# Attention, then two feed-forward layers on one core: an opening with paired heads in a written order, the first step's points spread out

## The chip, the cores and the metric

The kernel runs on one core of a Trainium2 chip. The metric is device time of one execution in microseconds (us), the median of several runs. Work is done by TensorE (matrix products into the PSUM banks), VectorE, ScalarE, GpSimd (POOL in the rows) and by transfers that SyncE (SP) issues; each engine takes its instructions in the order in which they were written.

## The reference

Three layers follow each other. First chunked attention: 4 batches, 8 heads, 768 positions, head size 64; each chunk of 32 positions sees 8 memory keys, 16 positions to its left, itself and 8 to its right.

```python
for c in range(nc):
    k_full = np.concatenate([mem_k, k_ctx], axis=2)
    v_full = np.concatenate([mem_v, v_ctx], axis=2)
    scores = scale * np.matmul(q_c, k_full.transpose(0, 1, 3, 2))
    scores = scores - np.max(scores, axis=-1, keepdims=True)
    a = np.exp(scores)
    a = a / (np.sum(a, axis=-1, keepdims=True) + 1e-09)
    out[:, :, c_start:c_end] = np.matmul(a, v_full)
```

Its output, 3072 tokens of 512, goes through `relu(x @ w_in)**2 @ w_out` and then, with other weights, through `h * tanh(log1p(exp(h)))` between two such products. `w_in` is 512 x 2048, `w_out` 2048 x 512, all in float64 weights and float32 tokens.

## The kernel before

**Stages.** Tokens are cut into 3 blocks of 1024. A block's attention is done in 4 pairs p of tiles of 128 positions (these are the pairs with numbers below; paired heads are another thing); pairs 0 to 3 (`early(p)`) form the opening, ahead of everything else, and pairs 4 to 7 and 8 to 11 are attended beside the products of the block before. Then 48 steps follow, 24 for each layer, 8 (`NQ`) to a block: step s multiplies the block by 256 columns of `w_in`, applies the gate, and a step later multiplies the result by the matching rows of `w_out`.

**A step.** `product` (L514) computes one of seven products P1 to P7 of sums of blocks of the weights and of x (a Strassen-like scheme), 6 matmuls of 512 columns each, since operands are split into a rounded part and a rest. Their order is P1, P6, P5, P2, P7, P4, P3, onto three PSUM banks a, b, c: P1 and P2 share a, P6, P7 and P4 share b, P5 and P3 share c. P1's bank is copied to u1 by ScalarE before P2 adds onto it; u2 (L817), u3 (L836), c22 (L838), c21 (L844) and c12 (L849) are VectorE sums out of the banks. `gate` runs on ScalarE and the rest of its split on GpSimd (L528). `unit` (L569) multiplies the gated values of the step before by its second matrix, eight units of 6 matmuls, between the products.

**Points.** After each product and each unit `rest()` is called once: it flushes pending stores and does what a table `beside` has planned for that point, 15 points to a step. Step 0 has no units, so points 3 and 4, 7 to 9 and 12 to 14 are called directly after one another. Planned there: the loading and decoding of weights (`plan_w`: A and a decode's first part on ScalarE, D and d its VectorE parts L160, L163 and L164, S and s block sums, R and r rounding on ScalarE L201, L and l the rest on VectorE L207), and attention for later blocks (`plan_attention`): scores at its point 0, maxima at 1 and 2, exponentials (L403, ScalarE) at 3 and 4, normalization (L417, GpSimd) at 6, transposes (L425) at 12, their copy at 13, values (L447) at 16, copy 17, sums 18 (GpSimd), store 22. Pairs 4 to 7 start at point 4 of step 0, then every 24 points.

**The opening** works pair by pair: scores (L367), maximum L385 and subtraction L387 on VectorE, exponentials L399 on ScalarE, sums L411 and inversion L413, L414 on VectorE, normalization L417, transposes L425, copies L435, values L447, copies L459, four sums L466 to L469, and `place_x`, which rounds into x on ScalarE (L479) and writes the rest on VectorE (L480). For each of 4 head groups and 4 chunks the scores are two matmuls, one per head of a pair, on 64 of the 128 rows each; values likewise. `busy(n, i)` issues n dummy matmuls (L872) into bank i.

## Time and profile before

| | us |
|---|---|
| median of three runs | 1082.09 |
| the three runs | 1081.63, 1082.09, 1086.12 |
| the profiled execution's own time | 1084.58 |
| its span, first to last instruction | 1082.8 |
| first product of step 0 starts | 56.40 |
| step 2 starts | 103.64 |

A profile is one execution. Times of rows count from the start of its span; "x12" is the number of instructions that a row merges; the bracket at the end gives the engine's idle time before the row and what ended it.

### The profile page before, as it was taken

Reading aid. Unit: us, or ns where it says so; the run is one execution under the profiler, and the core shown is the slowest. Engines: PE = TensorE matmul, PEld = TensorE weight load, DVE = VectorE, ACT = ScalarE, POOL = GpSimd, SP = SyncE. Lnnn points to the kernel's source line nnn. Section 1 sums busy time; section 2 is a strip of 40 time slices with the busy share of each in tenths; the row PEclk is TensorE's granted clock in tenths of the full one; section 3 lists DMA queues with packets and bytes.
Section 4 is the critical chain, followed back from the end, with each engine's and each line's share of the span. In section 5 each row is a group of like instructions: output and inputs, shape, how many; then the busy total and the mean of one; then the engine's idle time right before and its main releaser. Section 6 shows DMA issues by size and latency. Waiting matters only on the chain.

```text
span 1082.8 us, 19892 instructions
## 1 busy us (share of the span) xinstructions
PE 1042.6 (96%) x7443; PEld 845.8 (78%) x7443; DVE 849.3 (78%) x1147; ACT 586.3 (54%) x1119; POOL 424.3 (39%) x327
## 2 busy tenths in 40 slices
PE   6879999998999999999999999999999999999998
PEld 3658778776778788788888888888888888888887
DVE  5688889869757676789998767787868878867777
ACT  2478667745665764665664654444364443453332
POOL 2224423422333333222232245545465453644443
PEclk9889999999999999999999999999999999999999
DMA  9657877698999998999999998899998899987452
GB/s 346 238 175 275 314 271 273 224 329 295 358 362 323 333 330 281 301 321 380 352 357 323 314 302 279 310 309 339 384 348 289 297 309 365 376 257 224 155 175 78
DMA packets 192143, 321.38 MB, mean 297 GB/s; under 512 B 13488, under 2 KB 151088, under 8 KB 188208
## 3 DMA queue, kind: packets, MB, share of 16 engines
q1 hardware_dynamic: 192048, 320.11, 85.0%
q8 instruction: 60, 0.98, 0.4%
q14 instruction: 35, 0.29, 0.1%
HBM read 228.04 MB, written 92.01 MB: 296 GB/s over the span
## 4 chain that ended last, share of the span: by engine, by line
PE 73%; DVE 10%; ACT 6%; DMA 6%; issue 3%; SPq 2%; POOL 1%; DVEq 0%; ACTq 0%; POOLq 0%
PE banks L514 34%; PE banks L604 20%; PE banks L569 14%; PE banks L447 2%; DMA xt<-xt_d 2%; ACT p L403 1%; DVE y L583 1%; DVE val L163 1%; DVE val L160 1%; DVE val L164 1%; DMA w1s<-w_d 1%; PE banks L367 1%; PE banks L647 1%; ACT r L534 1%; ACT r L533 1%
## 5 line engine op out<-in xcount | busy, mean ns | idle before, releaser
L514 PE MATMUL banks<-x,w1s 128*128 128x512 f32 x2016 | 496.2, 392 | 12.9 <-DVE u L836 5.2
L514 PEld LDWEIGHTS banks<-x,w1s 128*128 128x128 f32 x2016 | 377.9, 189 | 97.7 <-DVE u L836 7.7
L528 POOL TENSOR_TENSOR g<-r,g 128x512 fp32r<-128x512 f32 x190 | 264.0, 1397 | 478.6 <-ACT g L527 346.3
L569 PE MATMUL banks<-g,w2s 128*128 128x512 f32 x1152 | 277.5, 391 | 5.6 <-DVE y L583 4.3
L569 PEld LDWEIGHTS banks<-g,w2s 128*128 128x128 f32 x1152 | 214.6, 188 | 53.8 <-DVE y L583 5.5
L592 DVE TENSOR_TENSOR m<-banks,m 128x1024 f32<-128x1024 f32 (+1 forms) x145 | 175.5, 1214 | 50.8 <-PE banks L604 45.6
L604 PE MATMUL banks<-g,w2s 128*128 128x512 f32 x828 | 206.5, 389 | 0.0
L604 PEld LDWEIGHTS banks<-g,w2s 128*128 128x128 f32 x828 | 155.4, 188 | 32.4
L527 ACT CAST g<-r 128x512 fp32r<-128x512 f32 x190 | 115.7, 620 | 27.9 <-DVE r L555 23.4
L583 DVE TENSOR_TENSOR y<-banks,y 128x512 f32<-128x512 f32 x168 | 111.3, 681 | 21.0 <-PE banks L569 21.0
L528 POOL TENSOR_TENSOR g<-more,g 128x512 fp32r<-128x512 f32 x47 | 66.8, 1426 | 63.3 <-ACT g L527 42.2
L533 ACT ACTIVATE r<-r 128x512 f32<-128x512 f32 x72 | 45.4, 630 | 56.0 <-DVE r L844 40.2
L537 ACT ACTIVATE r<-r 128x512 f32<-128x512 f32 x48 | 30.3, 632 | 72.1 <-DVE r L844 37.3
L534 ACT ACTIVATE r<-r 128x512 f32<-128x512 f32 x96 | 60.8, 633 | 3.0
L160 DVE TENSOR_SCALAR val<-val 128x512 f32<-128x512 f32 x64 | 40.3, 630 | 18.8 <-ACT val L153 18.8
L226 DVE TENSOR_TENSOR val<-val,hi 128x1024 f32<-128x1024 f32 (+1 forms) x32 | 35.7, 1116 | 23.8 <-ACT hi L219 23.5
L219 ACT CAST hi<-val 128x1024 fp32r<-128x1024 f32 (+1 forms) x32 | 30.5, 952 | 39.1 <-DVE val L164 19.3
L153 ACT ACTIVATE val<-raw 128x512 f32<-128x512 f32 x64 | 40.4, 668 | 20.7 <-DMA w_d<-val 10.0
L810 ACT COPY u<-banks 128x512 f32<-128x512 f32 x48 | 28.3, 589 | 41.3 <-PE banks L514 41.3
L164 DVE SCALAR_TENSOR_TENSOR val<-raw,val 128x512 uint32<-128x512 uint32 x64 | 47.2, 737 | 2.2
L417 POOL TENSOR_TENSOR p<-p,sum 128x512 f32<-128x512 f32 x22 | 28.2, 1301 | 43.8 <-DVE sum L414 22.0
L836 DVE TENSOR_TENSOR u<-banks,u 128x512 f32<-128x512 f32 x48 | 33.0, 688 | 12.7 <-PE banks L514 9.9
(88 smaller groups left out, 1044.6 us busy)
## 6 DMA issues: line engine op xcount, KB each, us to landing
w1s<-w_d SPq DMA_DIRECT2D x280, 256.0 KB, 6.0
w2s<-w_d SPq DMA_DIRECT2D x229, 256.0 KB, 5.9
raw<-w_dram SPq DMA_DIRECT2D x64, 512.0 KB, 5.6
w_d<-w1s SPq DMA_DIRECT2D x8, 1792.0 KB, 7.4
x<-xs_d SPq DMA_DIRECT2D x14, 1024.0 KB, 11.1
v<-v_dram SPq DMA_DIRECT2D x24, 512.0 KB, 8.2
xt<-xt_d SPq DMA_DIRECT2D x21, 512.0 KB, 8.2
k<-k_dram SPq DMA_DIRECT2D x24, 368.0 KB, 7.2
```

Of the source, the lines that this page charges most:

```text
L153: nc.scalar.activation(out=val, in_=high.bitcast(FP32), func=ACTF.Prelu, scale=REBIAS, alpha=NEGATIVE)
L160: nc.vector.tensor_scalar(out=val, in0=val, scalar1=LIMIT, scalar2=-LIMIT * NEGATIVE, op0=ALU.min, op1=ALU.max)
L164: nc.vector.scalar_tensor_tensor(out=vb, in0=low, scalar=29, in1=vb, op0=ALU.logical_shift_right, op1=ALU.bitwise_or)
L514: nc.tensor.matmul(out=ps, lhsT=w[:, a, f:f + 128], rhs=x[:, xi, c, kk, :], start=start and i == 0, stop=stop and i == len(order) - 1, ski ...
L527: nc.scalar.copy(out=g[:, 0], in_=r)
L528: nc.gpsimd.tensor_tensor(out=g[:, 1], in0=r, in1=g[:, 0].bitcast(FP32), op=ALU.subtract)
L533: nc.scalar.activation(out=r, in_=h, func=ACTF.Relu)
L534: nc.scalar.activation(out=r, in_=r, func=ACTF.Square)
L569: nc.tensor.matmul(out=ps, lhsT=w[:, a, blk(f), d % 2 * 128:d % 2 * 128 + 128], rhs=g_t[s, (f, t)][:, c, :], start=i == 0, stop=i == len(o ...
L583: nc.vector.tensor_tensor(out=y, in0=ps, in1=y, op=ALU.add)
L592: engine.tensor_tensor(out=to, in0=in0, in1=in1, op=ALU.add)
L604: nc.tensor.matmul(out=bank(first + d), lhsT=w[:, a, 128 * d:128 * d + 128], rhs=g[:, c, :], start=i == 0 and blk not in ONTO, stop=i == 2 ...
```

## The change

The opening is rewritten, and the first two steps and the first planned attention are moved.

- The two heads of a pair are multiplied together: K is laid into zeroed tiles, block-diagonally (`pairs_k`), so that one matmul uses all 128 rows and gives both heads' 64 slots; the transposed probabilities are laid out in the same way (`pairs_p`) for the values. VectorE and GpSimd zero the tiles at the start, K is loaded in four transfers a pair and not two, and each half's probabilities are copied by two ScalarE instructions of 64 rows.
- Scores, softmax, sums, normalization, transposes, values and placing are called by halves, in one order written as a string: a letter for the work, then the pair and the half. `place_x`'s rest of pair 0 (l00, l01) goes to GpSimd, block sums of pair 2 too. There are fewer dummy matmuls.
- In step 0 each product is followed by two points (`tick`), and P2 comes second.
- The second matrix of step 0 is decoded from point 9 and not 4, and step 1's eight units stand after P7 (four) and after P3 (four).
- Pairs 4 to 7 are attended from point 10, every 23 points; transposes and what follows them stand one point later, as they already did for pairs 8 to 11.

```diff
+        for j in range(2):
+            for i in range(2):
+                r = slice(64 * i, 64 * i + 64)
+                nc.sync.dma_start(
+                    out=pairs_k[p % 2][j][r, i], in_=k[2 * p + j][r].rearrange("p (a s) -> p a s", a=4)
+                )
...
+    def lay_pairs():
+        both = pool.tile([128, 2, 2, 4, KCOLS], FP32, tag="w1_1", name="kk")
+        pairs_k.append([pool.tile([128, 2, 4, KCOLS], FP32, tag=f"y{j}", name="kk") for j in range(2)])
+        pairs_k.append([both[:, j] for j in range(2)])
+        pairs_p.extend(pool.tile([128, 4, 4, 2, 32], FP32, tag=f"g{4 + j}", name="pp") for j in range(2))
+        for n, engine in enumerate((nc.vector, nc.gpsimd)):
+            for j in range(2):
+                for i in range(2):
+                    engine.memset(pairs_k[n][j][64 - 64 * i:128 - 64 * i, i], 0.0)
+        for j in range(2):
+            for i in range(2):
+                nc.gpsimd.memset(pairs_p[j][64 - 64 * i:128 - 64 * i, :, :, i], 0.0)
...
+    def scores_pairs(p, j):
...
+        for hp in range(4):
+            for c in range(4):
+                nc.tensor.matmul(
+                    out=out4[32 * c:32 * c + 32, hp // 2, :, hp % 2],
+                    lhsT=q_t[p][:, j, hp, 32 * c:32 * c + 32],
+                    rhs=pairs_k[p % 2][j][:, :, hp, STRIDE * c:STRIDE * c + SLOTS],
...
+        if early(p):
+            for j in halves:
+                ps = s_ps.pop((p, j)).rearrange("p (a c s) -> p a c s", a=4, c=4)
+                for i in range(2):
+                    r = slice(64 * i, 64 * i + 64)
+                    nc.scalar.copy(out=pairs_p[j][r, :, :, i], in_=ps[r])
+            return
...
+                    for c in range(4):
+                        for i in range(2):
+                            nc.tensor.matmul(
+                                out=to[64 * i:64 * i + 64, :, 1 - j, 32 * c:32 * c + 32],
+                                lhsT=v_t[p][j][:, i, a, c, :],
+                                rhs=pairs_p[j][:, 2 * a + i, c],
+                            )
...
-            12 + late: lambda: transpose_p(p),
-            13 + late: lambda: (copy_pt(p), load_q(p + 1) if (p + 1) % PSB else None),
-            16 + late: lambda: values(p),
-            17 + late: lambda: copy_x(p),
-            18 + late: lambda: sums_x(p, nc.gpsimd),
+            13: lambda: transpose_p(p),
+            14: lambda: (copy_pt(p), load_q(p + 1) if (p + 1) % PSB else None),
+            17: lambda: values(p),
+            18: lambda: copy_x(p),
+            19: lambda: sums_x(p, nc.gpsimd),
...
-                units_of(((), (), (0, 1), (), (2, 3, 4), (5, 6, 7))[n])
+                units_of((((), (), (0, 1), (), (2, 3, 4), (5, 6, 7)), ((), (), (), (), range(4), range(4, 8)))[s == 1][n])
...
+        def tick():
+            rest()
+            if s == 0:
+                rest()
...
+            if s == 0:
+                product(s, P2, a, False, True)
+                tick()
+                gate(s, 0, 0, a, new_r(layer))
             product(s, P6, b, True, False)
-            rest()
+            tick()
...
+        work = {
+            "s": scores_pairs, "x": softmax, "e": exps, "u": total, "i": invert,
+            "n": lambda p, j: divide(p, j, on["PPPD"[p]]),
+            "t": transpose_p, "c": copy_pt, "v": values, "o": copy_x,
+            "m": lambda p, i: sums_x(p, on["PPPD"[p]], i),
+            "h": lambda p, half: place_x(p, half, 0),
+            "l": lambda p, half: place_x(p, half, 1, on["PDDD"[p]]),
+            "b": busy,
...
+            "b12,7 s00 s01 Q2 K2 W0 W1 V1 x00 x01 e00 b3,2 s10 u00 e01 s11 Q3 K3 V2 V3 u01 i0 x10 n00 n01"
+            " b5,4 t00 x11 e10 c00 b1,5 t01 u10 b1,6 s20 e11 c01 s21 x20 v00 u11 e20 v01 A0 i1 x21 n10 A1 o00"
+            " n11 b1,2 t10 D1 o01 e21 m00 b1,2 t11 c10 u20 u21 m01 h00 b2,2 v10 i2 c11 D0 s30 n21 h01 v11 n20"
+            " S0 R0 l00 t21 x30 o11 s31 c21 t20 x31 l01 o10 e30 b1,0 v21 S1 e31 c20 u31 u30 m10 R1 b3,0 v20"
+            " i3 n30 h10 m11 L0 b1,0 t30 o21 o20 n31 c30 m20 L1 b2,0 t31 h11 v30 l10 m21 c31 l11 h20 b2,0 v31"
+            " l20 o31 o30 h30 m30 h21 l30 m31 l21 h31 l31 b9,0"
...
-                plan_w(s, 4, (0, s, 1), "A||a|D|d||R||L", round_w, split_w, "xt2")
+                plan_w(s, 4 if s else 9, (0, s, 1), "A||a|D|d||R||L", round_w, split_w, "xt2")
...
-            start, first, period = ((0, 4, 24), (NQ, 10, 22))[sb]
+            start, first, period = ((0, 10, 23), (NQ, 10, 22))[sb]
```

## Rows read from the trace of the kernel before

**Rows 1.** The profile page, busy time of each engine.

```profile
PE 1042.6 (96%) x7443; PEld 845.8 (78%) x7443; DVE 849.3 (78%) x1147; ACT 586.3 (54%) x1119; POOL 424.3 (39%) x327
```

**Rows 2.** Table by stages: PE, PEld, DVE, ACT, POOL busy, granted clock, DMA share, GB/s.

```profile
40.00:50.00 10.00, 7.77 (x146) 6.12 (x145) 7.82 (x14) 4.42 (x8) 0.00 (x0) 0.68 0.70 249
...
600.00:700.00 100.00, 100.00 (x443) 82.81 (x442) 75.96 (x87) 52.29 (x78) 45.99 (x33) 1.00 0.89 298
```

**Rows 3.** Timeline of TensorE, opening to step 2: start, length, line, count.

```profile
6.86 1.63 PE L367 MATMUL banks<-k,q 64*32 64x64 f32 x128
...
16.77 1.04 PE L425 MATMUL banks<-cst,p 128*128 128x128 f32 x8
...
20.23 2.06 PE L447 MATMUL banks<-pt,v 64*64 64x32 f32 x124 [0.17 <-ACT pt L435]
...
59.94 4.72 PE L514 MATMUL banks<-x,w1s 128*128 128x512 f32 x12 [1.81 <-ACT x L479]
...
78.30 2.93 PE L514 MATMUL banks<-x,w1s 128*128 128x512 f32 x6 [4.09 <-DVE r L844]
...
103.64 4.24 PE L514 MATMUL banks<-x,w1s 128*128 128x512 f32 x18
```

**Rows 4.** The chain that ended last, step 0: start, length, instruction.

```profile
72.36 4.86 ACT p L403 x32
```

**Rows 5.** The waits from 100 to 340 us: total, times, longest.

```profile
PEld banks L425 <- POOL p L417: 4.0, 4, 1.3
```

**Rows 6.** Timelines of SP and ScalarE in steps 6 and 7.

```profile
218.53 0.42 SPq L473 DMA_DIRECT2D xt_d<-stage  x1
...
222.47 0.33 SPq L137 DMA_DIRECT2D w_d<-w1s  x1
...
227.08 2.94 SPq L267 DMA_DIRECT2D xt<-xt_d  x2
...
237.12 1.05 ACT L281 CAST x<-xt 128x1024 fp32r<-128x1024 f32 x1 [8.59 <-DMA xt<-xt_d]
```

**Rows 7.** Timeline of VectorE, opening and step 0.

```profile
8.52 0.69 DVE L385 TENSOR_REDUCE mx<-banks 128x8 f32<-128x512 f32 x1 [6.59 <-PE banks L367]
...
11.18 1.47 DVE L411 TENSOR_REDUCE sum<-p 128x8 f32<-128x512 f32 x2
...
12.89 0.25 DVE L414 RECIPROCAL sum<-sum 128x16 f32<-128x16 f32 x1
...
59.92 1.23 DVE L480 TENSOR_TENSOR x<-stage,x 128x1024 fp32r<-128x1024 f32 x1 [1.11 <-ACT x L479]
61.06 0.42 DVE L160 TENSOR_SCALAR val<-val 128x512 f32<-128x512 f32 x1
...
62.59 0.68 DVE L817 TENSOR_TENSOR u<-banks,u 128x512 f32<-128x512 f32 x1
```

**Rows 8.** Timeline of GpSimd, opening and step 0.

```profile
13.29 2.04 POOL L417 TENSOR_TENSOR p<-p,sum 128x512 f32<-128x512 f32 x2 [12.85 <-DVE sum L414]
...
25.67 0.72 POOL L466 TENSOR_TENSOR stage<-stage 128x256 f32<-128x256 f32 x1 [3.99 <-ACT stage L459]
...
69.69 1.29 POOL L528 TENSOR_TENSOR g<-r,g 128x512 fp32r<-128x512 f32 x1 [29.79 <-ACT g L527]
```

**Rows 9.** The transfers of the first 30 us.

```profile
DMA packets 3485, 10.57 MB, mean 352 GB/s; under 512 B 523, under 2 KB 651, under 8 KB 3482
```

**Rows 10.** Timeline of ScalarE, opening and step 0.

```profile
19.12 1.05 ACT L435 COPY pt<-banks 128x512 f32<-128x512 f32 x2
...
51.05 3.46 ACT L479 CAST x<-stage 128x768 fp32r<-128x768 f32 x4
...
59.79 1.23 ACT L153 ACTIVATE val<-raw 128x512 f32<-128x512 f32 x2
```

**Rows 11.** Weight loads of scores and values, opening: count, ns minimum/median/maximum.

```profile
L367 PEld LDWEIGHTS banks<-k,q x512: 102/106/173, 6.8 to 38.1; 64*32 64x32 f32 x171
...
L447 PEld LDWEIGHTS banks<-pt,v x512: 129/135/223, 19.7 to 53.2; 64*64 64x64 f32 x171
```

More of the change, by code (lines that the diff above doesn't have):

```diff
@@ L435, in copy_pt, with values @@
             nc.scalar.copy(out=pt_t[p][:, h2], in_=ps.rearrange("p (j a s) -> p j a s", j=2, a=2))
-    def values(p):
+    def values(p, *halves):
         x_ps = s_ps[p] = bank(6), bank(7)
+        if early(p):
+            for j in halves:
+                for a in range(2):
+                    to = x_ps[a].rearrange("p (b j s) -> p b j s", b=2, j=2)
+                    for c in range(4):
+                        for i in range(2):
+                            nc.tensor.matmul(
+                                out=to[64 * i:64 * i + 64, :, 1 - j, 32 * c:32 * c + 32],
+                                lhsT=v_t[p][j][:, i, a, c, :],
+                                rhs=pairs_p[j][:, 2 * a + i, c],
+                            )
+            return
         for j in range(2):
@@ L451, in values, with copy_x @@
                             )
-    def copy_x(p):
-        x_ps = s_ps.pop(p)
-        tag = f"w2_{p % 2}" if early(p) else "at1"
-        st = stage_t[p] = pool.tile([128, 8, 2, 128], FP32, tag=tag, name="stage")
+    def copy_x(p, *halves):
+        x_ps = s_ps[p]
+        if p not in stage_t:
+            tag = f"w2_{p % 2}" if early(p) else "at1"
+            stage_t[p] = pool.tile([128, 8, 2, 128], FP32, tag=tag, name="stage")
+        st = stage_t[p]
+        if early(p):
+            for a in halves:
+                nc.scalar.copy(
+                    out=st[:, 0:4].rearrange("p (j a) b s -> p j a b s", j=2)[:, :, a],
+                    in_=x_ps[a].rearrange("p (b j s) -> p j b s", b=2, j=2),
+                )
+            return
         for par in range(2):
@@ L764, in units_of @@
         def units_of(n):
-            for i in n:
-                if prev:
-                    unit(s - 1, i // 4, i % 4, rest)
-                else:
-                    rest()
+            for i in n if prev else ():
+                unit(s - 1, i // 4, i % 4, rest)
         def multiply2(n):
@@ L822, in step @@
             product(s, P5, c, True, False)
-            rest()
+            tick()
             if second:
@@ L826, in step @@
             wait_point(2)
-            product(s, P2, a, False, True)
-            rest()
-            gate(s, 0, 0, a, new_r(layer))
+            if s:
+                product(s, P2, a, False, True)
+                tick()
+                gate(s, 0, 0, a, new_r(layer))
             if second:
@@ L841, in step @@
             product(s, P4, b, False, True)
-            rest()
+            tick()
             c21 = new_r(layer)
@@ L853, in step @@
             wait_point(5)
+            if s == 0:
+                rest()
             if layer == 1 and s < STEPS - 1:
@@ L939, in tile_chunk_attention_moe_moe2 @@
-        split_w(e, 1)
-        flush()
-        place_x(0, 3, 7)
-        normalize(3, nc.vector)
-        turn(2)
-        multiply(2)
-        busy(3, 0)
-        turn(3)
-        multiply(3, (1, 0, 3), (1, 3, 7), (2, 0, 3), (2, 3, 7))
-        busy(12, 0)
-        place_x(3, 3, 7)
-        load_raw(2)
+        for name in "Q0 K0 Q1 K1 V0".split():
+            load_first[name[0]](int(name[1]))
+        flush()
+        e = (0, 0, 0)
+        on = {"P": nc.gpsimd, "D": nc.vector}
+        work = {
+            "s": scores_pairs,
+            "x": softmax,
+            "e": exps,
+            "u": total,
+            "i": invert,
+            "n": lambda p, j: divide(p, j, on["PPPD"[p]]),
+            "t": transpose_p,
+            "c": copy_pt,
+            "v": values,
+            "o": copy_x,
+            "m": lambda p, i: sums_x(p, on["PPPD"[p]], i),
+            "h": lambda p, half: place_x(p, half, 0),
+            "l": lambda p, half: place_x(p, half, 1, on["PDDD"[p]]),
+            "b": busy,
+            "A": lambda h: rebias(e, h, "val"),
+            "D": lambda h: decode(e, h),
+            "S": lambda i: sums_w(e, i),
+            "R": lambda i: round_w(e, i),
+            "L": lambda i: split_w(e, i),
+            **load_first,
+        }
@@ L951, in tile_chunk_attention_moe_moe2 @@
+        for name in (
[6 rows of a table added]
+        ).split():
+            work[name[0]](*(int(i) for i in (name[1:].split(",") if "," in name else name[1:])))
+        load_raw(2)
+        flush()
         load_k(PSB)
```

156 lines of the change are left out of this document (64 added, 92 removed).

## The prediction

> **What bounds the kernel now.** I read the page first: TensorE is busy for 96% of the span [rows 1], so a change helps only where TensorE waits or runs at the lower clock. The table by stages says where: from 600 to 700 us it is busy in every microsecond and nothing moves there, while in the opening (up to the first product at 56.4) its work is dummy products and small attention products, and the granted clock averages 0.68 of 2.4 GHz from 40 to 50 us, so part of that time is at 1.2 [rows 2]. The timeline of TensorE then shows what the real work waits for: product P6 of step 0 starts at 59.94 and P6 of step 1 at 78.30, after 4.09 us of waiting for VectorE's L844 [rows 3]. That instruction stands behind a softmax sum that needs the 4.86 us of exponentials on ScalarE [rows 4]. From 78.3 to 103.64, where step 2 begins, TensorE is full. So two stretches can give time: the opening, and steps 0 and 1. Two later places touch the moved attention: waits of the transposes for GpSimd [rows 5], and step 7, where ScalarE idles 8.59 us for the next group's x [rows 6].
>
> **Cost of the new forms.** A score pass before is 128 records in 1.63 us, some 1.41 without the last one's way through the array, so 11 ns each, 64 rows and 64 columns. After: 64 records a pair, 128 rows and 128 columns. The 128-column transposes, on all rows, take 1.04 us for 8 with the last one's end, so about 0.11 us each at full speed, 64 columns half that [rows 3]. 55 ns against 11 ns means five score records at once; two row halves account for a factor of two, so at least 2.5 column strips run together. New score record: 110/2.5 = 44 ns at most, 110/4 = 27 at least; a half (32 records) 0.9 to 1.4 us. Values now take at most 17 ns a record; with all rows and 64 columns, two strips: 55/2 = 28 to 55 ns, a half 0.9 to 1.8 us. I take 1.05 for each, near the low end, because the score row shows strips overlapping. Per pair that is 4.2 us against 3.5 before: the change buys no TensorE time here, only halves that can start separately and half the instructions.
>
> Against this speaks a rule of the Trainium skill ("TensorE: Matmul & The Clock Gate", Part 3, Packing small matmuls: what overlaps): a weight load passes a running product only when their row groups differ, and paired heads use all rows each time. The transposes contradict it so far: all rows, new weights for each, yet 0.11 us apart. By the rule the sum would be that of rival 3.
>
> **Zeroing.** VectorE's four fills run from 2 us while the first K lands; scores began at 6.86 [rows 3]. No such fill is in the trace; a 1024-element x pass takes 1.23 us [rows 7], so four cost at most 4.9 us, just covered. GpSimd's eight, by its 1.02 us a normalization [rows 8] about 8 us, lie before its first normalization at 13.29. If the cover fails, it costs 1 to 2 us. K's extra eight transfers cost queue time only.
>
> **The opening, along its order.** Its chain starts with the scores of pair 2, whose K reuses pair 0's buffer. By bytes, the 4.8 MB up to that K take 13.6 us at the mean 352 GB/s of the first 30 us [rows 9], so it is in at 16 at the earliest; the kernel before starts its scores after the values of pair 0, which run from 20.23 to 22.3 [rows 3]. I take 19. Then:
> - scores half 1.05, maximum and subtraction 1.33 (two halves run from 8.52 to 11.18), sum 0.74, inversion 0.45 with the small addition [rows 7], hand-offs of some 0.05 each: 22.8.
> - GpSimd, in order: n10 n11 (2.2), m00 m01 (2.84), n21 n20 (2.2), l00 (2.1), l01 (2.8), m10 (1.42). From 1.0 a normalization, 0.72 a 256-element sum, 1.29 for 512 elements written rounded, so 1.29 times 1.5 and 2 for 768 and 1024 [rows 8], normalizations and x parts raised by some 8% for VectorE beside them: 13.6, to 36.4.
> - ScalarE: h10, o21 o20, c30, h11, c31: 0.75 + 1.0 + 1.0 + 0.93 + 1.0, from two 512-element copies in 1.05 and four x casts in 3.46 [rows 10]. A c now costs two copies, not one: 4 us more of ScalarE over the four pairs, on the chain only here. To 41.1.
> - v31 1.05, o31 o30 1.0, h30 0.75: 44.0 with the hand-offs; l30 1.1, then P1 starts at 45.2.
> - m31 0.72, l21 1.38, l31 1.38 on VectorE: 48.6, when P6's operand is ready.
>
> P2, now second, needs only the first blocks, but it adds onto P1's bank, so it waits for the u1 copy (0.55, half of two), queued behind h31 and the two decodes of point 0 (1.23) [rows 10]: 48.6. P6 follows at 50.1, against 59.94 [rows 3]: 9.8 us earlier, one product more already done.
>
> **Steps 0 and 1.** VectorE decodes from 48.6: two at 1.53, four sums in 1.6, a 768-element split 0.95, so u2 is done at 54.8 [rows 7]. P7 needs it: 1.8 us of TensorE idle. It ends at 56.3, u3 frees the bank for P4 at 57.0, scores run to 59.9, P3 to 61.3. VectorE: softmax, c21, D, softmax, d, c12 end at 65.8. ScalarE: c21's gate to 63.2, exponentials of one half (2.43 by [rows 4]) to 65.6, c12's gate to 67.7, second half to 70.1, then weight rounding 1.05, decodes 1.23, u1 0.55: 73.0. P1, P6 and, after c12, P5 of step 1 are through at 67.3; P2 adds onto u1's bank and waits for it: 5.7 us idle, a new wait in place of the 4.09. Units cannot fill it, since the change puts them behind P7. Left of step 1 from there: four products, eight units at 1.45 (18 matmuls cost 4.24 with the last end [rows 3]), transposes and values 3.0: 20.4, plus 1.4 for six matmuls at half clock (2.93 against 1.5, as at 78.30). Step 2 starts at 94.8. Before: 103.64 less the scores (1.41) that come later now, 102.2. The gain that reaches step 2 is 7.4 us. The later second matrix (decode from point 9, ready at 77 when the first unit starts at 77) costs nothing here; with 1 us more of VectorE delay it would cost that.
>
> **Group 2's attention**, first start six points later, period 23, transposes a point later: VectorE's and ScalarE's work per pair is unchanged. The transposes' waits for GpSimd, 4.0 us of weight-load time [rows 5], mostly go: bounds 0 and 4, I take 2.5, as matmuls in the array cover the rest. But the last pair's store falls four points later in its sums and three in its place: behind the weight store issued at 222.47 instead of at 218.53. The load of x at 227.08 came just when the store (8.4 us) had landed; the x landed 10 us later and freed ScalarE at 237.12 [rows 6]. Bounds: 0, if the load only moves from the transfers' queue into SP's, and 5.5, if the whole delay passes on. The store's 0.9 MB at 352 GB/s is 2.6; I take 2.
>
> **Sum.** 7.4 + 2.5 - 2 = 7.9 us off the profiled 1084.58 us: 1076.7. The median of the three runs is 2.5 lower (1082.09), so 1074.2; I say **1074.5**. About 0.5%, 5.4 us, is what a measurement can tell from no change.
>
> **Rivals.**
> 1. *Nothing measurable, opening at half clock.* With scores and values at 2.1 us a half TensorE becomes the opening's chain: P6's operand at 57.7 instead of 48.6, nine later, so about 1083. For it: 0.68 from 40 to 50 us and fewer dummy products after. Against: the products stand closer, since halves of two pairs alternate.
> 2. *The tail gives it back.* Step 7's full 5.5 and no transposes gain: 7.4 - 5.5 = 1.9, so 1080. For it: the load stands right behind the store's landing. Against: the writes it would queue behind drain meanwhile.
> 3. *Slower: strips do not overlap.* At 0.11 us a score record (3.5 us a half) and 55 ns for values (1.8), P6 comes at 66, 16 later than forecast: 1090. With each weight load in front of its product (106 and 135 ns, [rows 11]) it is 3.4 and 4.3 a half, P6 at 85, about 1109. It decides from some 2.3 us a half. The score row (five at once) and the transposes speak against. It is the rule above, by which the time would be that last one.
> 4. *More than forecast.* K of pair 2 at 17, GpSimd unslowed, no wait in step 1 at P2: 6 us more, 1068.
>
> **Chances.** Forecast 0.53 (own range 1070 to 1079), rival 1 0.13, rival 2 0.12, rival 3 0.12 (0.07 of it by the weight loads), rival 4 0.10. Faster (below 1076.7): four fifths of the first (0.42), rival 4 (0.10), a little of rivals 1 and 2 (0.03), so 0.55; slower, rival 3 alone, 0.12; same 0.33. The range is 1067 to 1084: below it half of rival 4 (0.05), above it rival 3 (0.12) and a little of rival 1 (0.03).
>
> **What would show it.** P1 near 45 and P6 near 50; score halves near 1.05 us; GpSimd busy almost throughout 23 to 36 us; P2 of step 1 held near 73 by ScalarE; step 2 at 95; the transposes of pairs 6 and 7 without idle; step 7's x at most 2 us later relative to its first product. It is wrong if score halves take over 2 us, if the granted clock stays near half beyond 40 us, or if the lead at step 2 is lost by step 8.

## The result and the profile after

The changed kernel takes **1093.56 us** (median of four runs, 1092.42 to 1096.82) against 1082.05 for the kernel before on the same chip: a ratio of 1.0098, 95% interval 1.008 to 1.0117. It is slower by 11.5 us where 7.6 less were forecast, and the time lies outside the range. The profiled execution has 1094.67 us and a span of 1092.8, 10.0 longer than before's 1082.8; the rest of this document accounts for those 10.0.

The page after: the busy times, and the queue that brings instructions (packets, MB, share).

```profile
PE 1040.6 (95%) x6890; PEld 845.5 (77%) x6895; DVE 852.1 (78%) x1145; ACT 593.1 (54%) x1127; POOL 437.4 (40%) x341
...
q8 instruction: 55, 0.90, 0.3%
```

TensorE has 553 matmuls fewer and 2.0 us less work than in [rows 1]. So it does not work longer; it waits longer, or works at the lower clock. The table by stages of after, the opening and two late stretches (columns as in [rows 2]):

```profile
0.00:10.00 10.00, 6.48 (x77) 3.18 (x77) 4.65 (x7) 1.28 (x1) 5.11 (x12) 1.00 0.83 205
10.00:20.00 10.00, 5.24 (x87) 3.44 (x82) 6.68 (x12) 4.84 (x8) 2.04 (x2) 1.00 1.03 290
20.00:30.00 10.00, 7.75 (x140) 5.87 (x141) 5.68 (x10) 4.23 (x8) 3.16 (x4) 0.83 1.04 335
...
300.00:350.00 50.00, 46.27 (x553) 37.68 (x552) 25.70 (x45) 31.69 (x78) 14.11 (x13) 0.93 0.94 328
...
600.00:700.00 100.00, 100.00 (x443) 82.71 (x442) 72.87 (x85) 53.25 (x79) 41.68 (x30) 1.00 0.90 304
```

The same two stretches of the kernel before, for the last two columns:

```profile
10.00:20.00 10.00, 6.51 (x156) 3.88 (x154) 7.96 (x16) 4.40 (x8) 2.58 (x3) 1.00 1.02 392
20.00:30.00 10.00, 6.83 (x264) 4.77 (x263) 6.66 (x12) 2.14 (x5) 4.50 (x6) 0.83 1.03 408
```

The transfer engines are as busy as before (1.02 to 1.04) and move 290 and 335 GB/s in place of 392 and 408. A finer table of after tells where: 227 GB/s ahead of pair 2's K, whose scores start at 22.04, and 416 behind it.

```profile
18.00:20.00 2.00, 0.00 (x0) 0.00 (x0) 0.00 (x0) 1.82 (x4) 0.00 (x0) 1.00 1.04 227
...
24.00:26.00 2.00, 2.00 (x37) 1.30 (x39) 1.86 (x3) 0.44 (x1) 0.00 (x0) 0.67 1.04 416
```

From 600 us on TensorE is full in both kernels: all is decided earlier. The timeline of TensorE after ("issue" in a bracket means that the profile shows nothing that the engine waited for):

```profile
12.57 1.08 PE L384 MATMUL banks<-kk,q 128*32 128x128 f32 x32 [1.67 <-DMA kk<-k_dram]
...
22.04 1.93 PE L384 MATMUL banks<-kk,q 128*32 128x128 f32 x32 [4.36 <-DMA kk<-k_dram]
...
30.24 1.15 PE L509 MATMUL banks<-pp,v 128*64 128x64 f32 x32 [0.29 <-ACT pp L493]
...
44.69 1.15 PE L509 MATMUL banks<-pp,v 128*64 128x64 f32 x32 [3.88 <-ACT pp L493]
...
54.12 1.19 PE L603 MATMUL banks<-x,w1s 128*128 128x512 f32 x4
...
59.99 7.09 PE L603 MATMUL banks<-x,w1s 128*128 128x512 f32 x24 [3.77 <-ACT u L900]
...
78.16 1.66 PE L603 MATMUL banks<-x,w1s 128*128 128x512 f32 x6 [2.79 <-DVE r L944]
85.03 5.39 PE L603 MATMUL banks<-x,w1s 128*128 128x512 f32 x12 [5.22 <-ACT u L900]
...
97.19 2.93 PE L658 MATMUL banks<-g,w2s 128*128 128x512 f32 x6 [2.66 <-ACT y L670]
...
111.44 4.24 PE L603 MATMUL banks<-x,w1s 128*128 128x512 f32 x18
...
303.52 2.06 PE L522 MATMUL banks<-pt,v 64*64 64x32 f32 x127
309.07 0.31 PE L522 MATMUL banks<-pt,v 64*64 64x32 f32 x1 [3.48 <-issue]
309.31 5.49 PE L658 MATMUL banks<-g,w2s 128*128 128x512 f32 x12
```

P1 starts at 54.12, 2.3 earlier than before, not 11. P2, now second, waits 3.77 for u1, and P6 comes behind it. Step 1's P2 starts at 85.03 after 5.22, and its 12 matmuls take 5.39 us, 2.88 at full clock. Step 2 starts at 111.44: against [rows 3], with the one score pass (1.41) that now lies behind it taken off, 102.23, that is 9.2 later. The other 0.8 arise behind step 2: the transposes' idle for GpSimd [rows 5] is gone, but one idle of 3.48 us that no engine releases has come, after 127 of 128 records of a values pass, and 12 matmuls at the lower clock behind it (5.49 us, 2.88 at full clock).

What stands behind the waits in the opening and in step 0, on VectorE, GpSimd, SP and ScalarE after:

```profile
35.75 1.94 DVE L175 TENSOR_TENSOR val<-val 128x256 f32<-128x256 f32 x1
37.73 2.46 DVE L176 TENSOR_TENSOR val<-val 128x256 f32<-128x256 f32 x1
```

```profile
35.13 4.77 POOL L570 TENSOR_TENSOR x<-stage,x 128x768 fp32r<-128x768 f32 x2
```

```profile
48.73 0.33 SPq L137 DMA_DIRECT2D w_d<-w1s  x1
49.16 0.37 SPq L137 DMA_DIRECT2D raw<-w_dram  x1
```

```profile
56.07 1.04 ACT L568 CAST x<-stage 128x1024 fp32r<-128x1024 f32 x1 [1.04 <-DVE stage L556]
58.24 1.22 ACT L153 ACTIVATE val<-raw 128x512 f32<-128x512 f32 x2 [1.12 <-DMA raw<-w_dram]
59.35 0.58 ACT L900 COPY u<-banks 128x512 f32<-128x512 f32 x1
...
84.36 0.62 ACT L900 COPY u<-banks 128x512 f32<-128x512 f32 x1
```

The raw weights of step 0's decodes are issued behind the store of w1 (48.73), because that store waits on SP for L207; they are decoded at 58.24, and u1 stands behind that decoding on ScalarE. Of u1's lateness this load is 1.12 us; up to 57.11 ScalarE was still placing x.

### The profile page after: what moved, and what is told of

It reads as the page before. It is cut to its first block, busy times and chain, and to the rows that moved or that the text cites. A ratio compares the mean times of both kernels' runs of the same rounds, so it can differ in the third digit from the quotient of the medians.

```text
span 1092.8 us, 18838 instructions
## 1 busy us (share of the span) xinstructions
PE 1040.6 (95%) x6890; PEld 845.5 (77%) x6895; DVE 852.1 (78%) x1145; ACT 593.1 (54%) x1127; POOL 437.4 (40%) x341
## 4 chain that ended last, share of the span: by engine, by line
PE 67%; DVE 13%; DMA 8%; ACT 6%; issue 3%; SPq 2%; POOL 0%; DVEq 0%; ACTq 0%; POOLq 0%
PE banks L603 31%; PE banks L693 20%; PE banks L658 13%; DVE val L164 2%; DVE val L163 2%; DMA raw<-w_dram 2%; DMA kk<-k_dram 1%; DVE y L672 1%; DVE val L160 1%; DMA w2s<-w_d 1%; DMA w_d<-hi 1%; ACT r L623 1%; SPq L253 1%; ACT r L622 1%; PE banks L736 1%
## 5 line engine op out<-in xcount | busy, mean ns | idle before, releaser
L658 PE MATMUL banks<-g,w2s 128*128 128x512 f32 x1152 | 283.0, 396 | 10.5 <-DVE y L672 6.1
L693 PE MATMUL banks<-g,w2s 128*128 128x512 f32 x828 | 206.5, 389 | 0.0
L160 DVE TENSOR_SCALAR val<-val 128x512 f32<-128x512 f32 x64 | 36.9, 576 | 23.2 <-ACT val L153 23.2
L164 DVE SCALAR_TENSOR_TENSOR val<-raw,val 128x512 uint32<-128x512 uint32 x64 | 48.6, 760 | 2.2
L911 DVE TENSOR_TENSOR u<-banks,u 128x512 f32<-128x512 f32 x48 | 32.8, 683 | 13.6 <-PE banks L603 7.7
## 6 DMA issues: line engine op xcount, KB each, us to landing
x<-xs_d SPq DMA_DIRECT2D x14, 1024.0 KB, 11.2
```

The source lines that it names most:

```text
L160: nc.vector.tensor_scalar(out=val, in0=val, scalar1=LIMIT, scalar2=-LIMIT * NEGATIVE, op0=ALU.min, op1=ALU.max)
L164: nc.vector.scalar_tensor_tensor(out=vb, in0=low, scalar=29, in1=vb, op0=ALU.logical_shift_right, op1=ALU.bitwise_or)
L658: nc.tensor.matmul(out=ps, lhsT=w[:, a, blk(f), d % 2 * 128:d % 2 * 128 + 128], rhs=g_t[s, (f, t)][:, c, :], start=i == 0, stop=i == len(o ...
L693: nc.tensor.matmul(out=bank(first + d), lhsT=w[:, a, 128 * d:128 * d + 128], rhs=g[:, c, :], start=i == 0 and blk not in ONTO, stop=i == 2 ...
```

## The experiments

Each time is a median, with its ratio to the kernel before on the same chip; "step 2" is the start of step 2 in the profile, with the difference to before (score pass adjusted where attention starts later). A place is read from one profile. P1 of the unedited opening lies at 55.64 to 57.84 in the five profiles that have it, so a difference of 2 us in the opening says little; the medians are of 4 to 12 runs.

### Which part costs it

**The opening alone** (old steps, old attention); `tick`'s second point and P2's place in step 0 are put back too:

```diff
-            start, first, period = ((0, 10, 23), (NQ, 10, 22))[sb]
+            start, first, period = ((0, 4, 24), (NQ, 10, 22))[sb]
-                plan_w(s, 4 if s else 9, (0, s, 1), ...)
+                plan_w(s, 4, (0, s, 1), ...)
-            13: lambda: transpose_p(p),
+            12 + late: lambda: transpose_p(p),
...
```

> The new opening with steps 0 and 1 and the second group's attention as before. Theory A (the rearranged steps 0 and 1 lose the time, the opening is about even): P1 near 54, P6 of step 0 near 58.5 against 59.94 before, step 2 near 102, so about 1080 to 1081. Rival B (the new opening is what costs, by its slower K transfers and what stands late behind it): P6 no earlier than 60, step 2 near 110, about 1090 or more.

1093.66, 1.0098 (1.007 to 1.0127): as slow as the whole change. But step 2 is only 1.4 late (105.08); 6.3 arise behind it, with idles without a releaser:

```profile
172.16 0.44 PE L522 MATMUL banks<-pt,v 64*64 64x32 f32 x9 [2.28 <-issue]
...
307.86 0.24 PE L522 MATMUL banks<-pt,v 64*64 64x32 f32 x1 [3.42 <-issue]
308.03 4.60 PE L658 MATMUL banks<-g,w2s 128*128 128x512 f32 x12
```

**The steps alone** (old opening, all else as after):

```diff
-        lay_pairs()
...
-            work[name[0]](*(int(i) for i in (name[1:].split(",") if "," in name else name[1:])))
+        busy(12, 7)
+        attend(0)
+        normalize(0)
...
```

> The opening of before with the new steps 0 and 1 and the new attention points. Theory A: P1 at 56.4 as before, P2 held by the u1 copy to about 61.5, step 2 near 113, about 1093 to 1096. Rival B: step 2 near 104, within 3 us of 1082.

1091.38, 1.0072 (1.0048 to 1.0096). Step 2 at 112.47, 10.2 late, by the waits of after (5.23 and 2.67) and with P1 1.1 later behind an idle of 2.16 at 53.04. Behind step 2 its profile is 4.4 us shorter than before's (976.2 against 980.6), and it has no idle without a releaser there. So the two halves lose in different places: the steps ahead of step 2, the opening behind it.

**u1 ahead of the point** in steps 0 and 1:

```diff
-            tick()
+            if s > 1:
+                tick()
             u1 = ring("u", 3, [128, NB], FP32, "u1")
             nc.scalar.copy(out=u1, in_=a)
+            if s <= 1:
+                tick()
```

> The changed kernel with the u1 copy written before the planned points in steps 0 and 1, so that P2 no longer waits for decoding or exponentials. If the two waits of P2 for the u1 copy (3.8 and 5.2 us) are the loss itself: about 1085. Theory A' (they only stand where the next wait would stand: P7 needs u2, which VectorE gives at the same time as before, behind the decoding): 0 to 2 us less, 1091 to 1094.

1093.76, 1.0084 (1.0053 to 1.0115). The waits for u1 shrink to 1.4 and 1.9, and P7 waits 2.95 and 2.37 for u2 in their place; step 2 at 112.48. So with the units last u1's place in ScalarE's queue does not decide: P7 waits for u2 instead, and step 1's P5 starts at 78.61 where it does at 78.16 in after.

**Units and second matrix as before**, the rest as after:

```diff
-                units_of((((), (), (0, 1), (), (2, 3, 4), (5, 6, 7)), ((), (), (), (), range(4), range(4, 8)))[s == 1][n])
+                units_of(((), (), (0, 1), (), (2, 3, 4), (5, 6, 7))[n])
...
-                plan_w(s, 4 if s else 9, (0, s, 1), ...)
+                plan_w(s, 4, (0, s, 1), ...)
```

> The changed kernel with step 0's second matrix decoded from point 4 again and step 1's units in their old places (two before P2, three before P4, three at the end); P2 second, spread points and attention at point 10 stay. Theory A (units put last leave TensorE without work while P2 and P7 of step 1 wait): 5 to 8 us less, 1086 to 1089. Rival C (the exponentials of the attention at point 10 are what delays step 1, units or not): within 2 us of 1093.6.

1089.43, 1.0057 (1.0039 to 1.0074). Step 2 at 106.99, 4.4 earlier than after, though an idle of 1.52 without a releaser lies ahead of it. Step 1's P2 still waits for u1, which stands on ScalarE behind the exponentials (82.23 to 84.55) and two decodes:

```profile
86.33 4.61 PE L603 MATMUL banks<-x,w1s 128*128 128x512 f32 x12 [3.24 <-ACT u L900]
```

**The same edit the other way**, units and second matrix late in the kernel before:

```diff
-                units_of(((), (), (0, 1), (), (2, 3, 4), (5, 6, 7))[n])
+                units_of((((), (), (0, 1), (), (2, 3, 4), (5, 6, 7)), ((), (), (), (), range(4), range(4, 8)))[s == 1][n])
-                plan_w(s, 4, (0, s, 1), ...)
+                plan_w(s, 4 if s else 9, (0, s, 1), ...)
```

> The kernel before with one edit: step 0's second matrix decoded from point 9 and step 1's units put after P7 and P3. Theory A (units in their old places are TensorE's cover while P2 and P7 of step 1 wait for ScalarE and VectorE): step 2 starts 4 to 6 us later than 103.64, 1086 to 1090. Rival (the loss needs the attention at point 10 or P2 second): within 2 us of 1083.

1087.09, 1.0039 (1.002 to 1.0059). Step 2 at 108.58, 4.9 late, with a wait that was not there and a stretch at the lower clock. At the end of the profile 2.4 of the 4.9 are left (1085.2 against 1082.8):

```profile
86.21 4.36 PE L514 MATMUL banks<-x,w1s 128*128 128x512 f32 x12 [2.75 <-ACT u L810]
```

**New opening, P2 second and spread points alone**: in after, units and second matrix as in the edit before last, and

```diff
-            start, first, period = ((0, 10, 23), (NQ, 10, 22))[sb]
+            start, first, period = ((0, 4, 24), (NQ, 10, 22))[sb]
-            13: lambda: transpose_p(p),
+            12 + late: lambda: transpose_p(p),
...
```

> The changed kernel with units, second matrix and attention as before: of the new steps only P2 second and the spread points stay. At step 2 the opening alone stood 1.4 us behind the kernel before, with units back 4.8. If P2 second and the spreading cost those 3.4: step 2 near 106.5, 1089 to 1091. If the attention at point 10 costs them: step 2 near 105 with the scores, 1092 to 1094 as the opening alone (it loses the transposes' gain as well).

1086.8, 1.0038 (1.0024 to 1.0052). Step 2 at 103.64, where it was before: the spread points take back the opening's 1.4. One idle of 2.51 without a releaser stands at 298. The kernel of the units put back (4.8 late, 1.5 of them its idle) differs from this one by the attention alone (from point 10, transposes a point later): 3.3, and the wait of 3.24 for u1 is not in this kernel. By the medians the two differ by 2.6 with overlapping intervals, so the 3.3 rests on the two profiles.

### The opening

**K in 64 rows a transfer**, in the kernel before:

```diff
-            nc.sync.dma_start(out=k_t[p][:, j], in_=k[2 * p + j]...)
+            for r in (slice(0, 64), slice(64, 128)) if early(p) else (slice(0, 128),):
+                nc.sync.dma_start(out=k_t[p][r, j], in_=k[2 * p + j][r]...)
```

> The kernel before with the opening's K loaded in four transfers of 64 rows a pair in place of two of 128, nothing else. Theory K (a transfer into 64 rows keeps the transfer engines busy for more time per byte): 205 to 220 GB/s in the first 10 us against 257 and about 300 against 392 in the second, pair 2's scores 2 us later, total 0 to 3 us more. Rival (the changed kernel's lower rate comes from something else, the order of the loads): rates as before and the time too.

1088.29, 1.0042 (1.0024 to 1.0061): the transfers alone, without paired heads.

```profile
10.00:20.00 10.00, 7.32 (x156) 4.26 (x154) 7.99 (x15) 3.43 (x6) 2.04 (x2) 1.00 1.04 336
20.00:30.00 10.00, 6.19 (x261) 4.59 (x263) 6.19 (x13) 3.02 (x6) 5.04 (x6) 0.81 1.03 272
```

At an unchanged busy share the rate falls to 336 and 272 GB/s. The last piece of pair 2's K lands at 25.1 (20.6 before), its scores come at 25.07 (22.96) and P1 at 61.33 (56.40). Not all of these 4.9 are K's: idles without a releaser stand in this opening, 7.6 us in four, where before has 4.4 in two. Two of the four:

```profile
41.73 1.32 PE L368 MATMUL banks<-k,q 64*32 64x64 f32 x108 [2.63 <-issue]
...
57.08 0.65 PE L448 MATMUL banks<-pt,v 64*64 64x32 f32 x13 [1.90 <-issue]
```

Step 2 is at 106.56, 2.9 late, and the profile ends 0.5 earlier than before's: it is the fastest of the ten runs (1084.09), so the median's 5.3 is not laid out in it.

**The two halves of K on two queues**, in after:

```diff
-                nc.sync.dma_start(
+                (nc.sync, nc.scalar)[i].dma_start(
```

> The changed kernel with the two 64-row halves of each K issued on two queues (SP's and ScalarE's), so that both halves of the rows are written at a time. Theory K2 (a transfer into 64 rows is slow because it writes only half of the rows at a time): rates near 390 GB/s in 10 to 20 us, pair 2's scores at 19 to 20 and not 22.04, P1 2 to 3 us earlier; the total 0 to 3 us less, since step 0 still waits for its weights. Rival (the pieces themselves are slow): 290 GB/s and 22 us as now.

1098.8, 1.0143 (1.0124 to 1.0162): K moves no faster (253 GB/s from 10 to 20 us, 290 in after), its first scores start at 10.95 and pair 2's at 24.76. SP's queue is not what makes the pieces slow.

**l00 and l01 on VectorE**, in after:

```diff
-            "l": lambda p, half: place_x(p, half, 1, on["PDDD"[p]]),
+            "l": lambda p, half: place_x(p, half, 1, on["DDDD"[p]]),
```

> The changed kernel with pair 0's rests of x (l00, l01) on VectorE and not on GpSimd. Theory G (GpSimd's two long passes, 4.8 us, stretch VectorE's two block sums beside them from 0.85 to 4.4 us): the sums take under 1.2 us, VectorE gives back 3.2 and takes on 2.2, P1 1 to 4 us earlier than 54.1, total 0 to 3 us less because step 0 then waits for its weights. Rival: the sums stay long, P1 2 us later.

1096.27, 1.0114 (1.0085 to 1.0144). The block sums return to 0.43 and 0.42 us, which shows that GpSimd's pass stretched them (the next two, L178 and L179, take 0.94 and 0.95 here, and 0.41 and 0.42 in after). P1 comes at 54.41 all the same: VectorE now has the work itself.

**The opening alone, mended**: K on two queues, and the loads for step 0 and pair 4 moved up into the order, ahead of the w1 store:

```diff
-            " ... e30 b1,0 v21 S1 e31 ..."
+            " ... e30 b1,0 v21 W2 K4 V4 S1 e31 ..."
```

> The new opening with steps 0 and 1 as before, K on two queues, and the first loads for step 0 (weights, K and V of pair 4) issued before the weight store and not after it. If the opening alone lost by late K and by step 0's loads standing behind the store (q landing only at 63.4): P6 near 55, scores of pair 4 without a wait for q, step 2 near 100 against 103.64, 1080 to 1084; with waits for instructions like those of the opening alone (about 6 us after step 2) 1086 to 1090.

1090.21, 1.0067 (1.0042 to 1.0092). The wait for q is gone, but P1 comes at 59.79 and step 2 at 106.08. The loads moved up are not the reason: SP issues their K at 45.57, and pair 2's scores are late long before, by the K that comes on two queues:

```profile
27.27 1.93 PE L384 MATMUL banks<-kk,q 128*32 128x128 f32 x32 [5.68 <-DMA kk<-k_dram]
...
45.57 1.66 SPq L325 DMA_DIRECT2D k<-k_dram  x2
```

Why they start 2.5 later here than with the two queues alone (24.76) is open. So whether the early loads help with K on one queue was not tried.

### The transposes

**A point later**, in the kernel before:

```diff
-        late = int(p >= 2 * PSB)
+        late = 1
```

> The kernel before with one edit: transposes, copies, values and sums of pairs 4 to 7 one point later, the store where it was. If the waits of the transposes for GpSimd (0.9 + 0.5 + 0.9 + 0.3 us of idle, and 1.1 at the values) are worth what they last: 2.5 to 4 us less, 1078 to 1081. Rival (the store then lands too late for step 7, or the wait goes elsewhere): within 1 us of 1083.

1085.36, 1.001 (0.9993 to 1.0028): no gain. The waits for GpSimd are mostly gone in the profile, but a wait of 1.6 us for the copy of the transposed probabilities stands at 168.5.

### The idles that no engine releases

So far they stood behind step 2 in the kernels with the new opening and in none with the old. Ahead of step 2 the old opening has them too; the kernel before:

```profile
13.89 0.78 PE L367 MATMUL banks<-k,q 64*32 64x64 f32 x56 [1.37 <-issue]
...
26.67 0.57 PE L367 MATMUL banks<-k,q 64*32 64x64 f32 x23 [2.99 <-issue]
```

**64 small matmuls ahead of pair 2's scores**, in after, to move everything behind them along TensorE's stream:

```diff
+        def tiny(a, b):
+            for _ in range(10 * a + b):
+                nc.tensor.matmul(out=bank(7)[0:32, 0:32], lhsT=ones[:, 0:32], rhs=ones[:, 0:32], start=True, stop=True)
...
-            " ... b1,6 s20 e11 ..."
+            " ... b1,6 y64 s20 e11 ..."
```

> The changed kernel with 64 dummy matmuls of 32 columns (128 instructions of TensorE) where it idles before pair 2's scores. Theory F (the 3.5 us idle at 309 us inside a values pass, for which the profile shows no releaser, is TensorE waiting for its next block of instructions, because the pass begins and ends with a block; shifting the stream by half a pass removes it): no idle there, 4 to 6 us less, 1087 to 1090. Rival (the idle belongs to that place in the work, whatever stands before it): idle unchanged, 1093 to 1095.

1092.68, 1.0079 (1.0053 to 1.0105): by the median the same as after. The profiled execution, 1088.89, lacks the idle at 309 and is the fastest of the five, whose highest is 1094.1; whether the others have idles is not to be seen.

**The same 64 in the opening alone:**

```diff
-            " ... b1,6 s20 e11 ..."
+            " ... b1,6 y64 s20 e11 ..."
```

> The kernel of the new opening alone with 64 matmuls of 32x32 on 32 columns added ahead of pair 2's scores, which add work of no use and lengthen TensorE's stream. Theory F (the idles of 2 to 4 us that no engine releases hang on where a pass lies in TensorE's instruction stream): the three after step 2 (0.4, 2.3 and 3.4 us in the opening alone) are gone or lie elsewhere, and if all are gone the time is 1086 to 1089 us. Rival (they come from the loads or the throttle, at a place in time): they stay near 172 and 308 us, and the time stays at 1092 to 1094.

1085.93, 1.001 (0.9995 to 1.0026): 7.7 us less than the same kernel without the added work, and no difference from before. Of the 6.1 us of idles behind step 2, 1.9 are left, elsewhere (346 and 408); a new one of 1.77 stands in the opening (29.37).

**90 of them in the kernel before:**

```diff
+        tiny(90)
         attend(2)
```

> The kernel before with 90 matmuls of 32x32 on 32 columns added ahead of group 2's attention, work of no use that moves the rest of TensorE's stream by 180 instructions. Theory F: idles of 2 to 4 us without a releaser appear after step 2, in late passes of values or scores, though the opening is the old one, and the time is 1084 to 1089 us. Rival (the idles belong to the new opening itself): none over 1 us appears, and the time is 1082 to 1084.

1094.72, 1.0096 (1.0065 to 1.0128), more than was expected: the old kernel with a loss as large as the new one's. In the profile 6.1 of its 11.6 stand at step 2 already (109.71); what the added work alone costs there is seen in the next kernel. TensorE of this kernel:

```profile
148.76 0.42 PE L367 MATMUL banks<-k,q 64*32 64x64 f32 x23 [2.22 <-issue]
...
278.00 0.43 PE L367 MATMUL banks<-k,q 64*32 64x64 f32 x5 [3.38 <-issue]
...
320.07 0.44 PE L367 MATMUL banks<-k,q 64*32 64x64 f32 x26 [3.77 <-issue]
320.44 4.62 PE L569 MATMUL banks<-g,w2s 128*128 128x512 f32 x12
```

How many matmuls TensorE has done when each idle is on (table by stages from 0; the count in brackets):

```profile
0.00:148.70 148.70, 123.32 (x2128) 0.92 0.69 255
0.00:277.90 277.90, 243.57 (x3144) 0.95 0.75 270
0.00:309.60 309.60, 274.47 (x3394) 0.94 0.77 276
0.00:320.00 320.00, 281.10 (x3521) 0.95 0.77 279
```

The distances are 1016, 250 and 127: 8, 2 and 1 times 125 to 127. In the opening alone the counts are 1362, 1744 and 2756, distances of 382 and 1012, 3 and 8 times 126.5 to 127.3. Each matmul has a weight load, so the period is about 253 instructions.

**126 in place of 90**, a whole period:

```diff
-        tiny(90)
+        tiny(126)
```

> The kernel before with 126 matmuls of 32x32 on 32 columns ahead of group 2's attention in place of 90. The idles without a releaser stood 125 to 128 TensorE records apart or a whole multiple of that. Theory F with a period of about 126 records: the later passes lie as in the kernel before, no idle of over 1 us without a releaser is left after step 2, and the time is 1082 to 1087 us, though more useless work is done than with 90. Rival (any added matmuls slow this kernel): 1095 us or more.

1088.39, 1.0052 (1.0033 to 1.0071): 6.3 less than with 90, with 36 more to do, and each of its four runs (1086.71 to 1091.4) is faster than each of the four with 90 (1091.73 to 1099.15). No idle over 0.32 us without a releaser is left behind step 2, and from step 2 on its profile is 8.2 shorter than that one (976.5 against 984.7). The added work's own price stands ahead of step 2: VectorE's L844 releases step 1's P6 at 83.5 where it did at 78.30 [rows 3], 5.2 later, and step 2 starts 5.3 later (108.91). In the profile 2.6 of this reach the end (1085.4 against 1082.8), by the medians 5.2. (The expectation put the top at 1087.)

What moves then: the instruction queue of after and of the opening alone, in the one microsecond from 306 and from 305.

```profile
q8 instruction: 1, 0.02, 5.9%
```

```profile
q8 instruction: 1, 0.02, 6.0%
```

The traces of all twenty kernels hold 53 such idles of at least 0.4 us, each in a pass of short matmuls or within 20 matmuls behind one. In each of the 53 the last packet of that queue starts 2.2 to 2.7 us before TensorE goes on, 306.8 for 309.07 in after and 317.6 for 320.07 in the kernel with 90 among them. So the idles end at a nearly fixed time after the next block of instructions begins to move: TensorE waits for instructions.

### What is left when they are avoided

**P2 second, spread points and later transposes in the kernel before:**

```diff
-            12 + late: lambda: transpose_p(p),
+            13: lambda: transpose_p(p),
...
+            if s == 0:
+                product(s, P2, a, False, True)
+                tick()
+                gate(s, 0, 0, a, new_r(layer))
```

> The kernel before with three parts of the change alone: the second product second in step 0, the units of the points spread over the passes of steps 0 and 1, and the transposes of the pairs of group 2 a point later; the second matrix, the units and group 1's attention begin as before. If the 1.4 us of the spread points and the 2.5 us of the transposes add up, 1079 to 1081 us. Rival (the new opening was what made room for the spread points, and the transposes' gain is lost again behind): 1082 to 1086.

1087.2, 1.0027 (1.0008 to 1.0047): no gain. Step 2 at 105.60; P2 waits 3.4 for u1.

**New opening, spread points and the 64 small matmuls** (the kernel of the spread points with "y64" as above):

> The new opening with the spread points alone and 64 matmuls of 32x32 on 32 columns of no use ahead of pair 2's scores. The same 64 took 7.7 us off the median of the opening alone; the spread points took 6.9 us off it. If the spread points' part is the 1.4 us at step 2 and the rest of both is the same stall, 1082 to 1086 us; if the two add up, 1078 to 1081, and this is the fastest kernel yet.

1084.47, 1.0009 (0.9997 to 1.0021), step 2 at 103.01: 9.1 less than the change as it was made, and no difference from before.

**With the transposes later as well:**

```diff
-            12 + late: lambda: transpose_p(p),
+            13: lambda: transpose_p(p),
...
```

> The kernel of the spread points with the 64 shifting matmuls, and group 2's transposes a point later as in the change. If the 2.5 us of the transposes count once no idle without a releaser lies behind them, 2 to 3 us under the kernel without them; rival: the same within 1 us, as in the kernel before.

1085.01, 1.0023 (1.001 to 1.0036): no gain from them here either, though the profile is ahead of before's: step 2 at 101.34, 2.3 earlier.

```profile
101.34 4.24 PE L603 MATMUL banks<-x,w1s 128*128 128x512 f32 x18
```

The lead is 3.8 at step 13 and 0.5 at the end (1082.3 against 1082.8). Most of it goes at two waits that before does not have, 1.77 for VectorE's L163 at 407.19 and 0.96 for x at 929.94. So a lead at step 2 does not reach the end by itself, as a delay there does not in the kernels with the units last and with 126 matmuls (4.9 and 5.3 late at step 2, 2.4 and 2.6 at the end).

No kernel of this study beats the one before.

## Why the prediction was wrong

Three steps of the sum failed at step 2, where 7.4 us were to be gained and 9.2 are lost: the opening's chain, the units and the second matrix put late (costs "nothing here"), and the attention from point 10. A fourth cause, the instruction stream, had no step at all. The one rival on the slow side, 3, had its chance for a mechanism that did not occur, so the time came out slower by ways that no rival names.

**The new forms: right.** A score half takes 1.08 us and a values half 1.15 (12.57, 30.24) against 1.05, so rival 3 falls: 32 records on all rows with new weights each stand 34 ns apart, while each of the scores' weight loads is recorded with 110 ns (median), and the rule of the Trainium skill ("TensorE: Matmul & The Clock Gate", Part 3, Packing small matmuls: what overlaps), by which each weight load would stand in front of its product, does not hold for them. The zeroing was covered, as said.

**The opening's chain: the step that failed is its first, "by bytes, the 4.8 MB up to that K take 13.6 us at the mean 352 GB/s".** In slices of 2 us where K moves in 64-row pieces the rate falls to 205 to 235 GB/s, with the engines busy throughout; the sum priced the extra eight transfers at "queue time only". That is shown by the kernel before with K cut so: pair 2's K 4.5 us later by that alone (P1 is 4.9 later, in part by idles for instructions). Pair 2's scores came at 22.04, not 19. Behind that, its first half ran at the lower clock (1.93 us), GpSimd's "13.6, to 36.4" became 14.8, to 41.6, and the 8% for shared work was put on GpSimd alone, while VectorE's two block sums beside its L570 took 4.40 us in place of 0.85. P1 comes at 54.12, not 45.2, a lead of 2.3 us in place of 11.2; of these 8.9 the late K is 3.0, and how the rest divides was not tried one by one. Moving l00 and l01 away won nothing, so that second cause is no larger than the work that it saves.

**P2 second: the wait was named, and its size was off.** u1 was to come at 48.6, P6 at 50.1; u1 ended at 59.93. Of these 11.3 P1's own lateness is 8.9. The prediction queued u1 behind point 0's two decodes, and did not ask when the raw weights for them land: they are issued behind the w1 store, which waits for VectorE, and ScalarE waits 1.12 for them. So the opening's gain at P6, 9.8 by forecast, is none: P6 follows P2's six matmuls from 59.99, so not before 61.4, against 59.94 [rows 3].

**Steps 0 and 1.** P2 of step 1 waits 5.22 (5.7 forecast, right). But it does not simply come "in place of the 4.09": P5 ahead of it waits 2.79 for c12 (L944), where the forecast's own times leave some 1.5. And that the later second matrix "costs nothing here" is wrong: with the units behind P7 nothing fills TensorE in these waits, its clock falls (0.67 from 80 to 90 us), and the fourth unit waits 2.66 for y. These two alone cost 4.9 at step 2 in the old kernel; putting them back gains 4.4, with 1.5 lost to an idle for instructions, so 5.9. From point 10 the attention's exponentials stand in front of step 1's u1 on ScalarE: with the units in their old places 3.3 us, the wait of 3.24 for u1. (With the units last, u1 ahead of them won nothing.) By the profiles the 9.2 at step 2 are 0.0 (opening, P2 second and spread points together), 3.3 and 5.9.

**Group 2's attention.** The transposes' waits went, as forecast (2.5), and the time did not fall in the two comparisons with this one edit: the term belongs at 0. The delay of step 7 was priced at 2 and is 0: ScalarE waits 8.83 us for the next x and not 8.59 [rows 6], and TensorE's idles there are those of before.

**What no step had: the instruction stream.** The prediction took "half the instructions" for something bought. 1101 TensorE records fewer move all later passes against the blocks in which instructions arrive; where a block runs out in a pass of short records (11 to 34 ns each) or close behind one, TensorE stands up to 4 us and, behind several of these idles, works for some microseconds at the lower clock (in after 3.48 of idle and 5.49 where 2.88 is usual, 6.1 in all). This costs the opening alone 7.7 us by the medians. The kernel before has two such idles, 1.37 us at 13.89 and 2.99 at 26.67, both in the scores, and none behind step 2: the trace held them, and the forecast did not ask what they were. The Trainium skill ("Runtime: NRT & Kernel Launch", Instruction fetch mechanics) says that an engine's instructions are refilled in blocks of 256, mostly hidden. The period of some 253 agrees with the block; hidden it is not, in passes of this kind. Why the packet starts too late in some passes and in time in others (the transfer engines' busy share is 0.94 from 300 to 350 us) was not tried.

After's own 10.0 thus are 9.2 up to step 2, 6.1 from the idle at 309 with its stretch at the lower clock, less what is shorter behind step 2, 4.4 in the steps alone. That makes 10.9; the last 0.9 are not assigned. Of the 4.4 the transposes' idles are not all: some 2.5 of a delay at step 2 is taken up behind it also where the attention is that of before. So the sum had one more step without a reason, that a gain at step 2 reaches the end in full; the one kernel that had such a lead, 2.3, kept 0.5 of it.

By the ratios the way back goes from 1.0098 (after) to 1.0057 with units and second matrix put back, 1.0038 with the attention put back, and 1.0009 with the 64 small matmuls. The first and the last step are clear of the intervals, the middle one is not.

## What to carry to other kernels

Ask of every edit that changes the number of short matmuls where the later short passes come to lie in the instruction stream: look in the trace for idles inside a pass that no engine releases, and try a few dozen small matmuls before judging the edit, since 64 of them took 7.7 us off one kernel here, and another was 6.3 slower with 90 than with 126. Cutting a load into half-height pieces has a price in bandwidth, not only in queue time. And a product moved ahead of its cover needs a date for everything in front of its release, down to the load that a decode waits for. Do not count a lead early in the kernel as a gain before asking which later waits can take it.

## What the hardware showed that was not expected

- With K in transfers of 64 rows the rate fell to 205 to 235 GB/s in slices of 2 us, with the transfer engines fully busy; by stretches of 10 us it was 336 and 272 where it is 392 and 408 with 128 rows. A second queue did not help.
- TensorE's idles without a releaser lie 125 to 128 matmuls, each with its weight load, or a multiple of that, apart in every kernel that has two or more; each of 53 ended 2.2 to 2.7 us after a 0.02 MB packet of the instruction queue began. That queue carried 55 packets in after, and 61 in the kernel before with 126 matmuls added.
- 256-element sums on VectorE went from 0.42 to 1.94 and 2.46 us beside GpSimd's rounded 768- to 1024-element passes, and back to 0.43 when those were moved.
